# A recurrence and two expert layers on one core: another start list, a shorter unit, GpSimd in written order, spare PSUM for late conversions, a re-ordered last group

## The chip, the core and the metric

The kernel runs on one core of a Trainium2 chip. The core has five engines: TensorE (PE in the profile, PEld its weight loads), VectorE (DVE), ScalarE (ACT), GpSimd (POOL) and SyncE (SP), which issues most DMAs. The metric is device microseconds of one execution; before the change the median of 3 runs is 1033.3 us (1029.38 to 1034.28).

## The reference

Three stages follow one another. The first is a recurrence over 768 time steps for each of 4 x 8 heads with a 40 x 40 state; the second and third are dense layers on the 3072 x 320 result.

```python
for t in range(S):
    y[:, :, t] = np.einsum('bhd,bhde->bhe', rt, state)
    Sa = np.einsum('bhde,bhe->bhd', state, at)
    state_decay = state * wt[:, :, None, :] - np.einsum('bhd,bhe->bhde', Sa, bt)
    state = state_decay + np.einsum('bhd,bhe->bhde', vt, kt)
x = y.transpose(0, 2, 1, 3).reshape(B * S, H * D)
x = np.maximum(np.maximum(x @ w1, x @ w2), x @ w3) @ w_out     # 320 -> 768 -> 320
h = x @ w_in                                                   # 320 -> 2048
out = (h * np.tanh(np.log1p(np.exp(np.minimum(h, 20.0))))) @ w2_out   # h > 20: tanh(h)
```

The dense layers' weights come as 64-bit floats and are converted on the chip (`from64`: a test of the high words, then ScalarE, VectorE and GpSimd steps that put a 32-bit float together).

## The kernel before

**Recurrence.** The time axis is cut into 48 chunks of 32 steps (24 for each half of the batch). For two chunks at a time a *unit* (`pre`) makes what the chunk needs of its inputs alone: a scan of the decays on DVE (L281), its logarithm and inverse on ACT, the scaling of keys and b vectors on DVE (L310, L312), a product on POOL (L248), small matmuls on PE into `m` (L328), a copy of half of `m` to `ab` on ACT (L333), a transpose of the other half to `akT` on DVE (L336), and a masked selection on POOL (L343). In the generator `pre` a `yield` stands between the copy and the transpose. Four units make a batch, whose triangular systems are solved in 31 steps (`solve`: a product `tv`, L371, and a subtraction on `T`, L373): the first two batches on DVE, all others on POOL. A *chunk* (`chain`) is the serial part, five slots: `x0` (L449), `ups` (L462), `utps` (L472), the products into `cgps` (L416) with their mask `rs` on DVE (L483), and `ys` (L495) with the next state `sv` on DVE (L500). `kb` (L388) transposes a unit's keys on PE, four matmuls for each half, into one PSUM buffer that ACT empties into `ls` (L392).

**First dense layer.** It runs in 12 groups of 256 tokens beside the chunks. Products go to PSUM (`bps`, L743 to L747), the maximum of three is made by ACT and DVE (`mx`, L873, L875), its rounded part by ACT (`hh`, L877) and the rest by POOL (`hl`, L878); PE multiplies both by the second weights (L916), six pairs of `hh` and `hl` (hl0 to hl5) in a group, and ACT and DVE bring the result out (L905, L907). The generator of a group is advanced six times in a chunk.

**The order of the work.** Chunks 0 to 8 follow `START`, a list of 472 tokens written out: W, A, K, V and L are loads, u a step of a unit, c a slot of a chunk, e a solve step, w a step of a weight's conversion, k a half of `kb`, f a step of the first layer, m, s, l, Z memsets. There every engine and DMA queue works in that order. From chunk 9 `run` writes the order; PE, DVE and ACT keep it, while POOL and SP are ordered by the compiler's scheduler. In `run`, the solve steps of a batch are spread over the slots that are left to its due chunk (`steps` a slot).

**The tail.** After chunk 47 come the rest of the first layer's last groups together with conversions of the second layer's weights (`staged`, steps at L676 and L677 on DVE, L679 on POOL). `open_tail` gives the first layer a fourth PSUM bank. Then the second layer's six groups run (`Moe2.group`, 512 tokens each): 16 products `cps`, an activation chain on ACT and DVE (`e`, `r`, `gh`, `gl`), and 16 sets of output matmuls `cops` (L1093 to L1095). Then `gate.count` sums the counters of the range tests (matmul `g_p`, L171, reduction, cast to an integer `g_n`), and a branch on that number skips a general version of the program.

Of the kernel before, what the change touches and what calls it, by code (L numbers as in the profile page):

```python
# [17 lines left out]
C = 32  # L18
# [88 lines left out]
u4 w8 V2 c0 w11 w9 w13 u4 u5 w7 L2 w9 c1 A8 w8 w9 w10 w11 w10 k2 w14 w12 w10 u4 u5 x5 c1 w15 u5 w10 w11 u4 u4
w12 w16 c1 w13 w11 w12 w14 c1 w13 w17 w14 u4 w18 u4 w15 w13 c1 u5 w12 k3 V3 w14 u5 K7 w13 w15 w19 w14 u4 w16
u5 L3 w17 w17 u5 c2 w15 w16 w20 c2 u5 w18 c2 w15 w18 w19 u5 w17 w21 u5 c2 V4 c2 w18 k4 w17 u5 w19 w19 w20 c3
w18 w22 w23 w20 L4 w20 K8 w21 c3 w23 w19 w20 c3 w21 w23 w22 k5 w21 c3 w22 w23 w23 A9 u6 w21 V5 w16 c3 w16 L5  # L110
x6 w22 w22 c4 f20 u6 u6 c4 f21 u6 c4 u6 u6 u7 u7 c4 u7 V6 x7 f22 u6 u7 c4 K9 u7 u6 u6 u6 u6 L6 c5 f23 u7 u7 u7
# [11 lines left out]
class Gate:  # L123
# [26 lines left out]
    def count(self):  # L150
# [18 lines left out]
        with self.tc.tile_pool(name="g_ps", bufs=1, space=PSUM) as ps:  # L169
            p = ps.tile([1, len(runs)], F32, name="g_p")  # L170
            nc.tensor.matmul(out=p, lhsT=ones, rhs=cnt, start=True, stop=True)  # L171
            s = pool.tile([1, 1], F32, name="g_s")
            nc.vector.tensor_reduce(out=s, in_=p, op=ALU.add, axis=mybir.AxisListType.X)
# [5 lines left out]
class Attention:  # L179
# [93 lines left out]
    def pre(self, n):  # L273
# [60 lines left out]
        yield  # L334
# [255 lines left out]
    def run(self, fill):  # L590
# [333 lines left out]
class Moe2:  # L924
# [91 lines left out]
    def open_work(self, ctx):  # L1016
# [80 lines left out]
    def group(self, q):  # L1097

        tc, nc = self.tc, self.nc
        acc = self.acc = [self.psb.tile([128, DM], F32, name=f"cops{j}") for j in range(4)]  # L1100
        rest = iter(()) if q else self.conversions()
        under, self.begun = self.begun, []
        early = len(under)
        for m in range(16 + 3):
            if early <= m < 16 and (q, m) not in self.ps:
                self.product(q, m)
# [12 lines left out]
            with tc.issue_after(self.newest):  # L1119
                next(rest, None)  # L1120
                if m == 11:
                    finish(rest)
        del self.x[q]
        o = self.p2.tile([128, 4, DM], F32, name="o")
        ga, sb = divmod(2 * q, S // GT)
        for b2 in range(2):
            for i in range(2):
                j = 2 * i + b2
                if i:
                    nc.vector.tensor_copy(out=o[:, j], in_=acc[j])  # L1130
# [3 lines left out]
            nc.sync.dma_start(out=self.out[r0:r0 + 2 * GT].rearrange("(i p) d -> p i d", i=2), in_=o[:, b2:4:2])  # L1134
# [148 lines left out]
def program(tc, A, out, only=None):  # L1283
# [7 lines left out]
    with ExitStack() as c_mid:  # L1291
        keep = c_mid.enter_context(tc.tile_pool(name="keep", bufs=1, side="right"))
        moe2 = Moe2(tc, A, x1, out, gate)
        with ExitStack() as c_moe1:
            moe1 = Moe1(c_moe1, tc, A, xs, x1, gate)
            with ExitStack() as c_att:
# [5 lines left out]
                def fill(c, slot):  # L1302
# [18 lines left out]
                    if c >= HAND and (c > HAND or slot > 0) and slot in (1, 4):  # L1321
# [10 lines left out]
                with tc.manual_schedule(engines=IN_ORDER | {mybir.EngineType.Activation}):  # L1332
# [6 lines left out]
            moe1.open_tail()  # L1339
# [21 lines left out]
    n, total = gate.count()  # L1361
# [21 lines left out]
```

## Time and profile before

| | |
|---|---|
| runs shown | 1029.38, 1033.3, 1034.28 us |
| profiled execution, its own time | 1034.91 us |
| its span (first to last instruction) | 1033.2 us |
| TensorE clock granted, mean | 0.967 of full speed |
| busy: PE, DVE, ACT, POOL | 917.4, 752.2, 735.3, 479.4 us |
| chunk 0 starts, chunk 10 starts, second layer's steady part | 56.5, 206.9, 697 to 1016 us |

Busy shares are averages over stages with different limits. A chunk's length is read from one start of `x0` to the next; the clock column of the same stretch tells whether PE was slowed, and the idle time in brackets in front of an instruction tells what it waited for.

### The profile page before, as it was taken

The numbers are of one execution on the slowest core, as the hardware profiler recorded it, in microseconds if no ns is written. First come the engines' busy times: TensorE is split into PE (matmuls) and PEld (weight loads), VectorE is DVE, ScalarE is ACT, GpSimd is POOL, SyncE is SP. The second block draws the span as 40 slices with busy tenths as digits, with TensorE's granted clock in tenths as the row PEclk, the third lists the DMA queues.
The fourth block names the chain that finished last, engine by engine and source line by source line (L and its number), as shares of the span: only waits on it lengthen the run. The fifth ranks groups of instructions, "written<-read, shape, count | busy, mean of one in ns | idle before, by whom it ended". The sixth has DMA issues, their size and how long they took to land. (4 is left out here: it accounts for less than half of the span.)

```text
span 1033.2 us, 34141 instructions
## 1 busy us (share of the span) xinstructions
PE 917.4 (89%) x14098; PEld 824.6 (80%) x14098; DVE 752.2 (73%) x1411; ACT 735.3 (71%) x1858; POOL 479.4 (46%) x715
## 2 busy tenths in 40 slices
PE   3046778899999999999999999979999999999996
PEld 3034667798888888898988988969888999889985
DVE  8976788665564656565366666698998888898875
ACT  5466635575765667576688977878787978878874
POOL 8488706479659838963953434880202010020000
PEclk9999588899999999999999999989999999999999
DMA  9565522535354454445345454420100000000000
GB/s 233 148 182 160 134 51 65 152 95 150 92 139 118 114 148 106 118 113 139 94 129 151 124 140 150 118 66 1 57 1 31 26 32 26 24 33 1 26 1 29
DMA packets 117334, 96.07 MB, mean 93 GB/s; under 512 B 73316, under 2 KB 93412, under 8 KB 117172
## 3 DMA queue, kind: packets, MB, share of 16 engines
q1 hardware_dynamic: 116432, 93.59, 33.4%
q8 instruction: 113, 1.85, 0.8%
q14 instruction: 49, 0.40, 0.1%
q10 hardware_dynamic: 740, 0.23, 0.1%
HBM read 81.20 MB, written 12.58 MB: 91 GB/s over the span
## 5 line engine op out<-in xcount | busy, mean ns | idle before, releaser
L743 PE MATMUL bps<-bxh,bw 128*128 128x256 f32 x432 | 140.6, 326 | 4.5 <-ACT mx L873 3.4
L744 PE MATMUL bps<-bxl,bw 128*128 128x256 f32 x432 | 124.9, 289 | 3.1 <-DVE bxl L756 3.1
L745 PE MATMUL bps<-bxh,bw 128*128 128x256 f32 x432 | 123.7, 286 | 0.0
L1046 POOL CAST cxh<-cxl 128x512 fp32r<-128x512 f32 x15 | 13.1, 911 | 188.2 <-DMA cxl<-x 188.2
L743 PEld LDWEIGHTS bps<-bxh,bw 128*128 128x128 f32 x432 | 83.4, 193 | 13.3 <-ACT mx L873 4.0
L744 PEld LDWEIGHTS bps<-bxl,bw 128*128 128x128 f32 x432 | 84.2, 195 | 4.9 <-DVE bxl L756 4.9
L248 POOL TENSOR_TENSOR ax<-ax,pp 40x256 f32<-40x256 f32 x96 | 69.2, 739 | 37.1 <-DVE pp L281 24.0
L745 PEld LDWEIGHTS bps<-bxh,bw 128*128 128x128 f32 x432 | 84.1, 195 | 0.0
L483 DVE TENSOR_TENSOR rs<-cgps,cst 64x256 f32<-64x256 f32 x96 | 40.6, 423 | 58.2 <-PE cgps L416 56.1
L878 POOL TENSOR_TENSOR hl<-mx,hh 128x256 fp32r<-128x256 f32 x72 | 56.0, 779 | 52.6 <-ACT hh L877 46.4
L1089 DVE TENSOR_TENSOR gl<-e,gh 128x512 fp32r<-128x512 f32 x93 | 69.9, 752 | 14.4 <-ACT gh L1088 13.4
L500 DVE TENSOR_TENSOR sv<-ys,pp 40x320 f32<-40x320 f32 x92 | 44.9, 488 | 47.3 <-PE ys L495 45.8
L875 DVE TENSOR_TENSOR mx<-bps,mx 128x256 f32<-128x256 f32 x144 | 60.2, 418 | 24.6 <-ACT mx L873 13.7
L373 POOL TENSOR_TENSOR T<-T,tv 128x31 f32<-128x31 f32 (+15 forms) x124 | 73.7, 594 | 8.6
L916 PE MATMUL bps<-hh,bo 128*128 128x256 f32 x360 | 77.0, 296 | 0.6 <-ACT mx L873 0.6
L1077 ACT ACTIVATE e<-e 128x512 f32<-128x512 f32 x93 | 58.6, 630 | 25.4 <-DVE e L1075 25.0
L1081 DVE SCALAR_TENSOR_TENSOR e<-e,r 128x512 f32<-128x512 f32 x93 | 68.6, 737 | 8.7 <-ACT r L1079 8.6
L495 PE MATMUL ys<-rs,ls 128*40 128x72 f32 x1536 | 66.9, 247 | 8.5 <-DVE rs L483 4.2
L371 POOL TENSOR_TENSOR tv<-tr,T 128x31 f32<-128x31 f32 (+15 forms) x124 | 67.8, 547 | 11.1 <-DVE tr L364 2.6
L343 POOL TENSOR_SCALAR_AFFINE_SELECT ax<-akT 32x256 f32<-32x256 f32 x96 | 47.5, 494 | 51.5 <-DVE akT L336 47.3
L495 PEld LDWEIGHTS ys<-rs,ls 128*40 128x40 f32 x1536 | 58.0, 130 | 15.1 <-issue 4.9
L1074 ACT ACTIVATE e<-cps 128x512 f32<-128x512 f32 x93 | 54.7, 589 | 18.9 <-PE cps L747 18.8
(241 smaller groups left out, 3157.2 us busy)
## 6 DMA issues: line engine op xcount, KB each, us to landing
bk<-in_KB_dram SPq DMA_DIRECT2D x24, 448.0 KB
sv<-in_SV_dram SPq DMA_DIRECT2D x96, 80.0 KB
raw<-in_w_dram SPq DMA_DIRECT2D x18, 384.0 KB
again<-in_w_dram SPq DMA_DIRECT2D x27, 256.0 KB
w<-in_W_dram SPq DMA_DIRECT2D x21, 231.0 KB
v<-in_VT_dram SPq DMA_DIRECT2D x48, 96.0 KB
rs<-in_RT_dram SPq DMA_DIRECT2D x48, 96.0 KB
cxl<-x SPq DMA_DIRECT2D x12, 384.0 KB
```

Source lines behind the costliest of these rows:

```text
L248: self.nc.gpsimd.tensor_tensor(out=xv[:, h], in0=xv[:, h], in1=P[ro, h, 0:C], op=ALU.mult)
L371: eng.tensor_tensor(out=tv, in0=abT[:, s, s + 1:C].unsqueeze(2).to_broadcast([128, n, s + 1]), in1=T[:, s, 0:s + 1].unsqueeze(1).to_broadc ...
L373: eng.tensor_tensor(out=T[:, s + 1:C, 0:s + 1], in0=T[:, s + 1:C, 0:s + 1], in1=tv, op=ALU.subtract)
L495: nc.tensor.matmul(out=self.ys[64 * y:64 * y + 40, p, 0:72], lhsT=l[:, y, p], rhs=r_[:, :, 4 * (p % 4) + 2 * (1 - y) + p // 4], start=True ...
L743: nc.tensor.matmul(out=ps, lhsT=h[:, k], rhs=xh[:, k], start=(k == 0), stop=False)
L744: nc.tensor.matmul(out=ps, lhsT=h[:, k], rhs=xl[:, k], start=False, stop=False)
L745: nc.tensor.matmul(out=ps, lhsT=l[:, k], rhs=xh[:, k], start=False, stop=False)
L875: after(1, lambda ps=ps, mx=mx: nc.vector.tensor_tensor(out=mx, in0=ps, in1=mx, op=ALU.max))
L916: nc.tensor.matmul(out=pss[d][rows], lhsT=lhsT, rhs=rhs, start=first, stop=last)
L1077: nc.scalar.activation(out=e, in_=e, func=AF.Square, bias=1.0)
L1081: nc.vector.scalar_tensor_tensor(out=e, in0=e, scalar=1.0, in1=r, op0=ALU.add, op1=ALU.mult)
L1089: nc.vector.tensor_tensor(out=gl, in0=e, in1=gh.bitcast(F32), op=ALU.subtract)
```

## The change

The change makes seven edits.

1. Another START list: the same 472 tokens, permuted. W0 is the first load and K0 the ninth token; before, K0 was the first. In chunk 9 the two halves of `kb`, k10 and k11, no longer follow one another directly.
2. In `pre`, the `yield` between L333 and L336 stays only while START is being written out. In `run` a unit has one step fewer, and `akT` is issued a slot earlier.
3. In `run`, a batch gets no solve step in slot 0 of a chunk whose number divides by 4.
4. POOL keeps the written order in `run` too, and the DMAs `again` are held in program order only there.
5. Past the last chunk, the first layer has three PSUM banks, and the fourth bank becomes the tile `words`, which takes the result of L676 and is read by L677.
6. The last group of the second layer makes its products a step earlier from m = 12, counts inside the group ahead of the output copies, gives three of four output copies to ACT and one to DVE, and sends one of the last two output DMAs from ACT's queue.
7. A condition in `tests` is written with the number 9 in place of HAND, which is 9.

```diff
 START = """
-m0 m1 K0 W0 W1 A0 W2 m2 A2 A1 K1 W3 K2 m3 A3 s1 V0 K3 w0 w1 w2 l1 s0 C l0 p R1 R0 u0 u0 u1 x0 u1 x1 u0 u0 u0
+W0 m1 m2 m0 W1 A2 A0 W2 K0 W3 V0 A1 K1 s0 K2 C m3 A3 s1 K3 w0 w1 w2 l1 p u0 u1 x0 u0 R0 u0 u0 u1 u0 u0 u0 R1
...
-    def count(self):
+    def count(self, psum):
...
+        p = psum[0:1, 0:len(runs)]
+        nc.tensor.matmul(out=p, lhsT=ones, rhs=cnt, start=True, stop=True)
...
         nc.scalar.copy(out=self.ab[:, i:i + 8], in_=psv[:, :, C:2 * C])
-        yield
+        if self.written:
+            yield
         akT = p1.tile([128, 4, 2, C], F32, name="akT")
...
                     steps = -(-left // max(1, 5 * (due - c) - slot - 2))
+                    if c > HAND and c % 4 == 0 and slot == 0:
+                        steps = 0
...
         self.tail = True
-        self.banks.append(self.pool("b_pt", 1, space=PSUM))
+        return self.pool("b_pt", 1, space=PSUM).tile([128, 512], I32, name="words")
...
-            self.tc.keep_in_program_order(dma)
+            if self.free:
+                self.tc.keep_in_program_order(dma)
...
-            if early <= m < 16 and (q, m) not in self.ps:
-                self.product(q, m)
+            for p in (m, m + 1)[:1 + (last and m >= 12)]:
+                if early <= p < 16 and p not in made:
+                    self.product(q, p)
+                    made.add(p)
...
+        if last:
+            self.passed = self.gate.count(self.psa.tile([128, self.N], F32, name="cps"))
...
-                if i:
+                if i and not (last and b2):
                     nc.vector.tensor_copy(out=o[:, j], in_=acc[j])
...
-                with tc.manual_schedule(engines=IN_ORDER | {mybir.EngineType.Activation}):
+                moe1.free = True
+                with tc.manual_schedule(engines=IN_ORDER | {mybir.EngineType.Activation, mybir.EngineType.Pool}):
...
-            moe1.open_tail()
+            moe2.stage.psum = moe1.open_tail()
...
-    n, total = gate.count()
+    n, total = moe2.passed
```

How the change moves instructions is shown at three places. The first is POOL around chunk 20, where the solve of a batch (`tv` and `T`) and the `hl` of a group of the first layer alternate. Before:

```order
L371 TENSOR_TENSOR tv_5364<-tr1_174,T0_161 128x255
L878 TENSOR_TENSOR hl4_4685<-mx_5162,hh4_4679 128x256
L373 TENSOR_TENSOR T0_161<-T0_161,tv_5364 128x17x15
L371 TENSOR_TENSOR tv_5413<-tr1_174,T0_161 128x256
L373 TENSOR_TENSOR T0_161<-T0_161,tv_5413 128x16x16
L371 TENSOR_TENSOR tv_5454<-tr1_174,T0_161 128x255
L373 TENSOR_TENSOR T0_161<-T0_161,tv_5454 128x15x17
L878 TENSOR_TENSOR hl5_4686<-mx_5303,hh5_4680 128x256
```

With the change:

```order
L883 TENSOR_TENSOR hl4_4687<-mx_5164,hh4_4681 128x256
L371 TENSOR_TENSOR tv_5364<-tr1_174,T0_161 128x255
L373 TENSOR_TENSOR T0_161<-T0_161,tv_5364 128x17x15
L883 TENSOR_TENSOR hl5_4688<-mx_5303,hh5_4682 128x256
L371 TENSOR_TENSOR tv_5451<-tr1_174,T0_161 128x256
L373 TENSOR_TENSOR T0_161<-T0_161,tv_5451 128x16x16
L371 TENSOR_TENSOR tv_5454<-tr1_174,T0_161 128x255
L373 TENSOR_TENSOR T0_161<-T0_161,tv_5454 128x15x17
```

hl4 now stands ahead of the step with 255 elements instead of in the middle of it, and hl5 two solve steps (four instructions) earlier than it did.

The second is DVE in chunk 17, where the first layer's split (L755, L756), its copy to the output (L907) and a unit's `akT` follow one another. Before:

```order
L755 TENSOR_SCALAR bxh,g_t<-bxl 128x768
L756 TENSOR_TENSOR bxl<-bxl,bxh 128x768
L907 TENSOR_TENSOR mx<-bps,mx 64x256
L336 STREAM_TRANSPOSE akT<-m_3558 128x2x4x32
L464 COPY ud<-ups 128x4x40
```

With the change:

```order
L757 TENSOR_SCALAR bxh,g_t<-bxl 128x768
L758 TENSOR_TENSOR bxl<-bxl,bxh 128x768
L336 STREAM_TRANSPOSE akT<-m_3558 128x2x4x32
L912 TENSOR_TENSOR mx<-bps,mx 64x256
L464 COPY ud<-ups 128x4x40
```

`akT` now stands ahead of the copy to the output, which has line L912 in the changed file.

The third is PE in chunk 9: the transposes of keys `kb`, and the first layer's `bps`. Before:

```order
L747 MATMUL bps<-bxl,bw_107 128x256
L472 MATMUL utps<-cst,ud 128x128 x2
L743 MATMUL bps<-bxh,bw_108 128x256
L744 MATMUL bps<-bxl,bw_108 128x256
L745 MATMUL bps<-bxh,bw_108 128x256
L743 MATMUL bps<-bxh,bw_108 128x256
L744 MATMUL bps<-bxl,bw_108 128x256
L745 MATMUL bps<-bxh,bw_108 128x256
L746 MATMUL bps<-bxh,bw_108 128x256
L747 MATMUL bps<-bxl,bw_108 128x256
L388 MATMUL kb<-cst,bk_150 128x104 x8
L416 MATMUL cgps<-rs_167,uT 32x32
```

With the change:

```order
L388 MATMUL kb<-cst,bk_150 128x104 x4
L472 MATMUL utps<-cst,ud 128x128 x2
L745 MATMUL bps<-bxh,bw_108 128x256
L746 MATMUL bps<-bxl,bw_108 128x256
L747 MATMUL bps<-bxh,bw_108 128x256
L745 MATMUL bps<-bxh,bw_108 128x256
L746 MATMUL bps<-bxl,bw_108 128x256
L747 MATMUL bps<-bxh,bw_108 128x256
L748 MATMUL bps<-bxh,bw_108 128x256
L749 MATMUL bps<-bxl,bw_108 128x256
L388 MATMUL kb<-cst,bk_150 128x104 x4
L416 MATMUL cgps<-rs_167,uT 32x32
```

The eight transposes that stood in one run are now two runs of four, with one `utps` and eight matmuls of the first layer between them.

## Rows read from the trace of the kernel before

**Rows 1.** Stretches of the span: busy time by engine, PEclk granted clock, DMA share.

```profile
100.80:155.00 54.20, 39.96 (x909) 34.84 (x912) 43.96 (x98) 29.40 (x87) 22.34 (x36) 0.72 0.40 97
697.00:1016.00 319.00, 318.66 (x1759) 287.14 (x1760) 278.20 (x456) 264.36 (x455) 29.80 (x25) 1.00 0.06 21
```

**Rows 2.** PE's waits, chunks 10 to 47 (206 to 624 us): total, times, longest.

```profile
PE kb L388 <- DVE akT L336: 4.0, 5, 1.0
PE bps L916 <- POOL hl L878: 3.2, 3, 1.5
...
PE cgps L416 <- ACT uT L475: 2.5, 3, 1.4
```

**Rows 3.** The same columns, single chunks: 9, 14, 15, 17, 18 and 20.

```profile
188.30:206.90 18.60, 15.46 (x327) 13.62 (x322) 10.72 (x20) 9.83 (x29) 6.76 (x11) 0.82 0.53 140
252.00:266.90 14.90, 13.10 (x283) 11.61 (x282) 5.91 (x13) 6.65 (x23) 13.63 (x24) 0.89 0.33 82
266.90:277.50 10.60, 10.60 (x227) 9.79 (x226) 7.44 (x13) 8.95 (x25) 9.16 (x18) 1.00 0.43 121
288.60:302.30 13.70, 12.38 (x231) 11.14 (x234) 10.05 (x18) 10.08 (x31) 7.70 (x16) 0.88 0.42 114
302.30:313.20 10.90, 10.90 (x287) 9.99 (x288) 5.82 (x13) 6.76 (x22) 9.89 (x17) 1.00 0.47 113
323.80:337.90 14.10, 12.68 (x283) 11.53 (x282) 6.46 (x14) 6.28 (x21) 13.06 (x19) 0.88 0.47 132
```

**Rows 4.** Timeline of POOL in chunk 20: start, duration, line, operation, tiles.

```profile
326.17 0.73 POOL L878 TENSOR_TENSOR hl<-mx,hh 128x256 fp32r<-128x256 f32 x1
...
328.08 0.62 POOL L371 TENSOR_TENSOR tv<-tr,T 128x256 f32<-128x256 f32 x1
328.78 0.73 POOL L373 TENSOR_TENSOR T<-T,tv 128x256 f32<-128x256 f32 x1
...
330.93 0.72 POOL L878 TENSOR_TENSOR hl<-mx,hh 128x256 fp32r<-128x256 f32 x1
```

**Rows 5.** Timeline of PE, chunks 17 and 20; idle time and releaser in brackets.

```profile
292.15 0.55 PE L388 MATMUL kb<-cst,bk 104*128 104x104 f32 x4 [1.02 <-DVE akT L336]
...
331.70 0.38 PE L916 MATMUL bps<-hl,bo 128*128 128x256 f32 x1 [1.42 <-POOL hl L878]
```

**Rows 6.** Timeline of DVE in chunk 17.

```profile
291.09 0.42 DVE L907 TENSOR_TENSOR mx<-bps,mx 64x256 f32<-64x256 f32 x1 [1.13 <-ACT mx L905]
```

**Rows 7.** Timeline of POOL in chunk 12.

```profile
230.47 1.19 POOL L878 TENSOR_TENSOR hl<-mx,hh 128x256 fp32r<-128x256 f32 x1
...
234.70 0.73 POOL L878 TENSOR_TENSOR hl<-mx,hh 128x256 fp32r<-128x256 f32 x1
```

**Rows 8.** Timeline of ACT in chunk 14.

```profile
258.96 0.37 ACT L873 COPY mx<-bps 128x256 f32<-128x256 f32 x1 [3.91 <-POOL hl L878]
```

**Rows 9.** Timeline of PE in chunk 9.

```profile
194.56 0.57 PE L388 MATMUL kb<-cst,bk 104*128 104x104 f32 x4 [0.64 <-DVE akT L336]
197.63 0.95 PE L388 MATMUL kb<-cst,bk 104*128 104x104 f32 x4 [2.50 <-ACT ls L392]
```

**Rows 10.** DVE's waits up to chunk 10 (0 to 206 us).

```profile
DVE rs L483 <- PE cgps L416: 9.9, 5, 4.4
...
DVE pp L281 <- DMA w<-in_W_dram: 1.5, 1, 1.5
```

**Rows 11.** Line L676 in the whole run: min/median/max ns, first and last start.

```profile
L676 DVE TENSOR_SCALAR bits<-raw x24: 485/552/561, 23.5 to 105.2; 128x384 int32<-128x384 int32 x18, 128x320 int32<-128x320 int32 x6
...
L676 DVE TENSOR_SCALAR t<-raw x13: 328/599/1424, 641.8 to 689.1; 128x320 int32<-128x320 int32 x7, 128x384 int32<-128x384 int32 x6
```

**Rows 12.** PE's waits between chunk 47 and MoE2's groups (624 to 700 us).

```profile
PE bps L916 <- POOL hl L878: 2.5, 1, 2.5
```

**Rows 13.** Timeline of the end.

```profile
1023.16 0.41 PE L1093 MATMUL cops<-c_cw,gh 128*128 128x320 f32 x1 [1.34 <-ACT gh L1088]
...
1026.54 0.14 DVE L175 CAST g_n<-g_s 1x1 int32<-1x1 f32 x1
```

More of the change, by code (lines that the diff above doesn't have):

```diff
@@ L107 @@
[L107 to L111, printed above, removed]
@@ new lines @@
+u2 x1 u2 l0 u1 u1 u2 u0 x2 u1 u1 u0 u1 u0 u0 u1 u1 u3 x3 u3 l2 u2 u2 u2 L0 u1 u3 u1 u3 z6 u3 u3 u2 u2 u2 u3 w0
+w3 L1 u2 u2 u3 w1 w1 u3 e0 w0 w4 w5 u3 z4 u3 z5 w2 K4 e0 A5 e0 w1 e0 e0 e0 A6 z7 e0 U A4 e0 w0 w0 A7 w2 w3 e0
+e0 w6 e0 e0 e0 w1 w4 w3 w3 w5 K5 e0 e0 e0 e0 e0 e0 w3 e0 e0 e0 w7 w2 w2 w4 w4 w5 w4 w6 e0 k0 k1 e0 w6 D w8 w5
+e0 w5 r K6 w9 w10 e0 V1 e0 e0 e0 e0 e0 e0 e0 e0 c0 w7 w7 Z0 c0 u4 w8 w8 u4 c0 w9 w11 w12 x4 w7 c0 u4 u4 w9 Z1
+w8 V2 w13 w11 c0 u4 w7 w8 L2 w9 c1 A8 w6 w11 w6 u5 w10 w10 u4 k2 w12 w10 x5 w13 u5 u5 u5 w10 w12 u4 u4 w14 w11
@@ new lines @@
+w11 w13 c1 c1 w9 c1 w15 w16 w17 u4 u4 w13 w13 V3 w14 w14 w18 w12 k3 w12 u5 u5 w15 c1 L3 w17 w15 w19 w14 w16 c2
+c2 w14 u4 w15 w18 w18 u5 c2 w17 w19 u5 w15 w16 w20 w21 c2 V4 w19 w18 u5 w17 u5 w19 w20 w18 u5 w22 w17 c2 k4
+w23 w20 c3 A9 L4 c3 w20 w21 w23 w19 w21 c3 w20 w22 w23 w22 w22 w21 k5 w23 c3 V5 w21 u6 w16 w22 w16 c3 L5 w23
+K7 c4 f20 u6 u6 c4 x6 u6 c4 u6 f21 u6 u7 u7 K8 c4 u7 u7 u6 c4 L6 u6 u7 u6 u6 x7 V6 u6 c5 u7 u7 u7 f22 f23 u7
+A10 f24 f25 K9 c5 u7 u7 e1 e1 e1 e1 e1 e1 c5 c5 e1 f26 f27 e1 e1 e1 V7 f28 k6 c5 L7 e1 e1 e1 e1 c6 c6 e1 c6 e1
@@ L168, in count @@
         nc.vector.memset(ones, 1.0)
[L169 to L173, printed above, removed]
+        p = psum[0:1, 0:len(runs)]
+        nc.tensor.matmul(out=p, lhsT=ones, rhs=cnt, start=True, stop=True)
+        s = pool.tile([1, 1], F32, name="g_s")
+        nc.vector.tensor_reduce(out=s, in_=p, op=ALU.add, axis=mybir.AxisListType.X)
         n = pool.tile([1, 1], I32, name="g_n")
@@ L802, in weights @@
             yield from64(self.nc, self.tmp, self.A["wo"][j], 1, DM, self.gate, lambda t, j=j: self.put_out(t[:, 0], j), later=True)
+    free = False
     def tests(self):
@@ L1099, in group @@
         tc, nc = self.tc, self.nc
+        last = q == 5
         acc = self.acc = [self.psb.tile([128, DM], F32, name=f"cops{j}") for j in range(4)]
@@ L1103, in group @@
         early = len(under)
+        made = {p for r, p in self.ps if r == q}
         for m in range(16 + 3):
-            if early <= m < 16 and (q, m) not in self.ps:
-                self.product(q, m)
+            for p in (m, m + 1)[:1 + (last and m >= 12)]:
+                if early <= p < 16 and p not in made:
+                    self.product(q, p)
+                    made.add(p)
             for i, g in enumerate(under):
@@ L1133, in group @@
             r0 = (2 * ga + b2) * S + sb * GT
-            nc.sync.dma_start(out=self.out[r0:r0 + 2 * GT].rearrange("(i p) d -> p i d", i=2), in_=o[:, b2:4:2])
+            (nc.scalar if last and b2 else nc.sync).dma_start(out=self.out[r0:r0 + 2 * GT].rearrange("(i p) d -> p i d", i=2), in_=o[:, b2:4:2])
 def any64(nc, pool, src, n, cols, out):
@@ L1320, in fill @@
                         next(groups, None)
-                    if c >= HAND and (c > HAND or slot > 0) and slot in (1, 4):
+                    if c >= 9 and (c > 9 or slot > 0) and slot in (1, 4):
                         next(tests, None)
```

12 lines of the change are left out of this document (4 added, 8 removed).

## The prediction

> **What bounds the kernel now.** I read the busy time by stretches first. From 697 us to 1016 us PE is busy 318.66 of 319 us at full clock [rows 1]; the change leaves the order there as it is, so these 319 us stay. Nothing that spares DVE, ACT or POOL there can be seen in the time. In the start it is otherwise: between 100.8 and 155 us PE is busy 39.96 of 54.2 us, and the clock column says 0.72 [rows 1], a mixture of the levels of 1.2 and 2.4 GHz. So there a gap costs twice: itself, and the slow work after it.
>
> The second view is PE's waits for chunks 10 to 47. Waits of PE are few: 4.0 us for `akT`, 3.2 us for `hl`, 2.5 us for `uT` [rows 2]. The third view, single chunks, tells what they cost. Chunks 15 and 18 have no gap, a clock of 1.00, and last 10.60 and 10.90 us; these I take as the floors of odd and even chunks. Chunks 14, 17 and 20 last 14.90, 13.70 and 14.10 us at 0.88 or 0.89 [rows 3]: 4.0, 3.1 and 3.2 us above them. Chunk 17 has one gap of 1.02 us in front of `kb`, chunk 20 one of 1.42 us in front of L916 [rows 5]. Here 2.44 us of gap go with 6.3 us of time, and the clock column says where the other 3.9 us are.
>
> **The change, part by part.** The profiled execution is the base: 1034.91 us, 1.7 us more than its span, 1.6 us over the median of the runs shown.
>
> *The unit's step.* In chunk 17, `akT` stands behind L907, which starts at 291.09 after DVE had waited 1.13 us for ACT [rows 6]; PE's `kb` waits for `akT`, since the buffer it needs is free only then [rows 5]. With `akT` ahead of L907, DVE does it in that idle time: 1.13 and 0.42 us earlier, more than the 1.02 us of the gap. What is late next is L907 by some 0.45 us, and its output transfer has nobody close behind. All five `kb` gaps, 4.0 us [rows 2], should go.
>
> *POOL in written order and no solve step in slot 0 of every fourth chunk.* At chunk 20 hl4 starts at 326.17 and hl5 at 330.93, after three pairs of solve instructions, one of which takes 0.62 + 0.73 = 1.35 us [rows 4]. hl5 is two pairs earlier after the change: 2 x 1.35 = 2.7 us, less what hl4's new place shifts (nothing: both stand ahead). The gap it ends is 1.42 us [rows 5]. So the two long `hl` gaps go, 2.9 of the 3.2 us [rows 2].
>
> Together 4.0 + 2.9 = 6.9 us of gaps. For the two chunks shown I take the measured 6.3 us; the remaining 4.5 us of gaps I price at 1.5 us for each, since among them one is as long as that of chunk 20 and the rest are 1 us or less: 6.7 us. That is **-13 us**. The bounds: at 1.0 for each us -6.9, at the ratio of 6.3 to 2.44 -17.8.
>
> *The first batch on POOL.* In chunk 14, ACT's copy `mx` waits 3.91 us for an `hl` that POOL has put behind other work [rows 8], PE then for ACT, and the chunk lasts 4.0 us over its floor. In written order that `hl` is done sooner. But in chunk 12 the fifth and sixth `hl` of a group, at 230.47 and 234.70 now [rows 7], come behind several more solve pairs of 1.35 us; I place them at about 236 and 238 us (an estimate from those rows), some 2 to 4 us after PE wants them. I take one new gap of 2 us with 1.5 us of slow clock against 4.0 us gained: **-0.5 us**, between -4.0 (no new gap) and +4 (the gap is 4 us at the same price, twice).
>
> *The list.* W0 goes first. DVE waits 1.5 us for it at its first scan [rows 10], behind K0's transfer, and DVE is what fills the start: -1.5 us. In chunk 9 `kb` waits 0.64 us for `akT` and, for its second half, 2.50 us for ACT, which must first empty the one buffer behind a logarithm and an exponential [rows 9]. The chunk lasts 18.6 us at 0.82 [rows 3], 8 us over the odd floor. With eight matmuls between the halves ACT has that time; I count half of the 8 us: -4. What the rest of the permutation does to the waits of the start the trace can't tell. DVE's largest there is `rs` for `cgps`, 9.9 us in five [rows 10]: half of it more or less is the bound on either side. **-5.5 us**, between -15 (the whole 8 us, 1.5, and half of 9.9) and +5.
>
> *The tail.* Three banks instead of four let PE's products wait sooner for ACT's copies. Most of this would be absorbed where PE waits 2.5 us for `hl` anyway [rows 12]. And L676 writes PSUM. Thirteen such steps lasted 328 to 1424 ns in SBUF, with a median of 599, while 24 steps that wrote PSUM (`bits`) lasted 485 to 561, with a median of 552 [rows 11]. The spread is what a neighbour makes of it, and the PSUM form has next to none. By medians 13 x 0.047 = 0.6 us of DVE are saved, and more where long steps stand in a chain. I take **-1 us**, between -4 and +3.
>
> The Trainium skill (VectorE: DVE Perf Modes, section "Why PSUM operands drop a tier") says that an operand in PSUM keeps VectorE from using both of its SBUF read ports for one tensor, so that 32-bit data goes at the plain rate: by it `words` makes each of these steps slower than the 328 ns form. The rows agree as far as they show: 552 against 328 ns at the shortest. By that rule alone the sum would get 13 x 0.22 = 2.9 us of DVE more, not 0.6 less; against it stands the median of 599 ns, which the SBUF form has beside busy neighbours. The same skill (SBUF, State Buffer, section "Who interferes with whom") calls the ports that VectorE shares with GpSimd an exclusive lock, which fits a maximum of 1424 ns.
>
> *The end.* PE waits 1.34 us for the last `gh` [rows 13]; with products one step ahead, the last activation chain runs under matmuls: -1.3. The count's cast now ends at 1026.68 us, and 6.5 us follow in which no view shows an instruction: the read of the number, the branch and the last transfers. With the count ahead, the read can begin where the last set of `cops` ends. That set of 12 matmuls begins at 1023.16 [rows 13]; at 319 us for 6 x 16 sets with their products, a set's own part is under 2 us [rows 1], so the read begins near 1025.1, 1.6 us sooner: -1.6. Together **-2.9 us**, between -1.3 (the last output's transfer sets the end) and -4.
>
> Sum: -13 - 0.5 - 5.5 - 1 - 2.9 = -22.9, so 1034.9 - 22.9 = 1012 us; less 1.6 us to stand at the median: I take **1010 us**.
>
> **The rivals.**
> - *`hl` held back by solve steps in every batch.* The scheduler could slip `hl` between solve instructions when its data was there; in written order it can't. POOL is busy 13.06 of 14.1 us in chunk 20 [rows 3], so it has hardly any slack. If POOL lags behind the written slot by more than 2 to 3 us at hl4, chunks 12, 20, 28 and 36 get the gap of chunk 12 (about 5 us with the clock) and, behind it, that of chunk 14 (4.0 us): 4 x 9 = 36 us, less the 11 us that such gaps cost now, less some 10 of the other gains: 1034.9 + 15 = **1050 us**. Against it: the empty slot 0 gives POOL two pairs of room just there, and POOL is at 9.89 of 10.9 us in chunk 18.
> - *The gaps move on.* What PE no longer waits for at `kb` and L916 it waits for at `uT` (2.5 us now [rows 2]) or at the split of the first layer; the chunk is bound by its own serial slots. Then the end's 2.9 us and the start's first 1.5 to 4 remain: **1028 us**. For it: ACT's copies and POOL are both close to full in these chunks. Against it: chunks 15 and 18 reach the floor with the same work.
> - *The list does more.* Half of the start's clock loss and DVE waits go too: -18 instead of -5.5: **999 us**. For it: PE is busy only 39.96 of 54.2 us at 0.72 between 100.8 and 155 us. Against it: the steps of chunks 0 to 8 stand at nearly the same places of the list.
> - *The tail gets worse.* `words` is one tile, so each conversion's L676 waits for the L677 before it, and three banks hold PE up: +7 instead of -1, **1019 us**.
>
> **How the numbers follow.** A measurement of this kernel tells 0.5%, 5.2 us, from no change. The forecast has 0.54, held-back `hl` 0.08, moved gaps 0.14, a better list 0.16, a worse tail 0.08. Faster than 1028.1: nearly all of forecast, list and tail, and a third of the moved gaps, 0.80; slower than 1038.5: the held-back `hl` and a little for a list that lengthens the start, 0.09; 0.11 between. With the terms' ends all on one side the sum would be 990 or 1039; the ends are not met together, so I take the better list on one side and the moved gaps on the other: 997 to 1028 us, which leaves out the held-back case and a few hundredths at each end.
>
> **What would show it.** Right: no wait of `kb` for `akT` after 206 us; chunks 17 and 20 at 11 us and clock 1.00; chunk 9 without its 2.50 us gap; the last `cops` set without the 1.34 us; `g_n` ahead of the output copies. The new gap of chunk 12 should stand there as L916 waiting for `hl`. Wrong: `hl` waits of over 2 us in chunks 20, 28 and 36, a chunk 0 that starts later than 56.5 us, or a second layer that starts as late as now though the chunks are shorter.

## The result and the profile after

The changed kernel takes 1020.81 us (1019.93 to 1021.82, 4 runs) against 1033.74 us (1029.38 to 1034.28, 4 runs), a ratio of 0.9884 with an interval of 0.9856 to 0.9913. That is 12.9 us less, inside the range of 997 to 1028, and a little over half of what was forecast. Its profiled execution took 1021.82 us, with a span of 1020.1.

The table cuts the spans of both profiles at the same places: the first `x0` matmul of chunks 10, 16 and 47, the end of the last `cops` matmul, and the end.

| us | start to chunk 10 | chunks 10 to 15 | chunks 16 to 46 | chunk 47 to last `cops` | to the end |
|---|---|---|---|---|---|
| before | 206.93 | 70.58 | 346.40 | 401.27 | 8.02 |
| changed | 206.54 | 73.83 | 336.03 | 397.37 | 6.34 |
| difference | -0.4 | **+3.3** | **-10.4** | -3.9 | -1.7 |

So chunks 16 to 46 gain, the first batch of chunks loses, and the start gives nothing in this execution. In the start DVE waits less for W0, but now it waits for the keys, whose load K0 was the first load before and is the ninth token now. DVE's waits up to 57 us in the changed kernel, to be held against the 1.5 us of [rows 10]:

```profile
DVE bk L309 <- DMA bk<-in_KB_dram: 2.1, 1, 2.1
...
DVE pp L280 <- DMA w<-in_W_dram: 0.4, 1, 0.4
```

Chunk 0 begins at 56.86 us, 0.4 us later than before. PE's waits in chunks 10 to 47 of the changed kernel, with the columns of [rows 2]:

```profile
PE bps L921 <- POOL hl L883: 4.8, 1, 4.8
...
PE cgps L416 <- ACT uT L475: 1.4, 3, 0.6
```

The line of `kb` for `akT`, 4.0 us in five [rows 2], is gone, and the waits for `hl` have become a single one of 4.8 us. Single chunks, with the columns of [rows 3] (9, 12, 14, 17 and 20):

```profile
190.50:206.50 16.00, 13.97 (x323) 12.79 (x322) 11.46 (x20) 10.37 (x31) 8.31 (x10) 0.89 0.60 156
...
228.50:248.00 19.50, 14.72 (x284) 13.19 (x282) 5.82 (x11) 6.00 (x20) 17.46 (x25) 0.74 0.31 86
...
258.80:269.70 10.90, 10.90 (x284) 10.00 (x282) 6.32 (x14) 6.81 (x23) 9.70 (x19) 1.00 0.45 112
291.40:302.80 11.40, 11.04 (x227) 9.87 (x226) 9.73 (x17) 9.42 (x29) 8.08 (x16) 1.00 0.56 150
325.10:336.00 10.90, 10.90 (x284) 10.02 (x282) 5.97 (x12) 5.96 (x20) 10.15 (x14) 1.00 0.57 152
```

Chunks 14, 17 and 20 have lost their long gaps and their slow clock. Chunk 12 had no long gap in the kernel before:

```profile
228.60:240.20 11.60, 11.28 (x283) 10.17 (x282) 6.14 (x13) 6.62 (x22) 10.82 (x16) 1.00 0.55 151
```

Now it lasts 19.5 us at 0.74, with POOL busy 17.46 us of it. The timeline of POOL there, in the changed kernel, shows why:

```profile
229.44 3.62 POOL L247 TENSOR_TENSOR ax<-ax,pp 40x256 f32<-40x256 f32 x4
...
237.36 0.72 POOL L883 TENSOR_TENSOR hl<-mx,hh 128x256 fp32r<-128x256 f32 x1
...
239.38 0.72 POOL L883 TENSOR_TENSOR hl<-mx,hh 128x256 fp32r<-128x256 f32 x1
```

The two `hl` that started at 230.47 and 234.70 us [rows 7] now start at 237.36 and 239.38 us, behind solve steps and the product L247. PE waits for the first of them (timeline of PE, changed kernel):

```profile
238.14 0.58 PE L921 MATMUL bps<-hl,bo 128*128 128x256 f32 x1 [4.78 <-POOL hl L883]
```

The new first words of the conversions in the tail, against the row of `t<-raw` in [rows 11] (line L678 of the changed file). Eleven of the thirteen steps write PSUM; the last two stay in SBUF, and the longest, 1421 ns, is the same step as the one of 1424 ns before:

```profile
L678 DVE TENSOR_SCALAR words<-raw x11: 481/497/561, 633.0 to 658.8; 128x320 int32<-128x320 int32 x6, 128x384 int32<-128x384 int32 x5
L678 DVE TENSOR_SCALAR t<-raw x2: 896/1158/1421, 666.2 to 675.9; 128x384 int32<-128x384 int32 x1, 128x320 int32<-128x320 int32 x1
```

The step behind it reads these words. Line L677 before, L679 in the changed kernel:

```profile
L677 DVE SCALAR_TENSOR_TENSOR t<-raw,t x13: 476/546/987, 642.2 to 691.9; 128x320 int32<-128x320 int32 x7, 128x384 int32<-128x384 int32 x6
...
L679 DVE SCALAR_TENSOR_TENSOR t<-raw,words x11: 471/489/555, 634.2 to 662.0; 128x320 int32<-128x320 int32 x6, 128x384 int32<-128x384 int32 x5
```

And the end of the changed kernel, where the idle time in front of the last `cops` set [rows 13] is gone and the output copies are the last work that shows:

```profile
1011.75 0.42 PE L1099 MATMUL cops<-c_cw,gh 128*128 128x320 f32 x1
...
1013.38 1.08 ACT L1144 COPY o<-cops 128x320 f32<-128x320 f32 x3 [1.68 <-PE cops L1101]
1013.67 0.49 DVE L1142 COPY o<-cops 128x320 f32<-128x320 f32 x1 [1.25 <-PE cops L1101]
```

### The profile page after: what moved, and what is told of

Its sections match the earlier page's. It is cut to its first block, busy times and chain, and to the rows that moved or that the text cites. A ratio compares the mean times of both kernels' runs of the same rounds, so it can differ in the third digit from the quotient of the medians.

```text
span 1020.1 us, 34113 instructions
## 1 busy us (share of the span) xinstructions
PE 916.0 (90%) x14098; PEld 825.4 (81%) x14098; DVE 748.2 (73%) x1410; ACT 736.0 (72%) x1859; POOL 476.5 (47%) x715
## 4 chain that ended last, share of the span: by engine, by line
PE 72%; DVE 12%; ACT 7%; DMA 3%; POOL 3%; issue 3%; SPq 0%; ACTq 0%; DVEq 0%; POOLq 0%
PE bps L745 6%; PE bps L921 5%; PE cops L1099 5%; PE cops L1100 5%; PE cops L1101 5%; PE ys L495 5%; PE bps L746 4%; PE cps L745 4%; PE bps L747 4%; PE cps L746 4%; PE cps L747 4%; PE cgps L416 2%; PE m L327 2%; PE ups L462 2%; PE bps L748 2%
## 5 line engine op out<-in xcount | busy, mean ns | idle before, releaser
L247 POOL TENSOR_TENSOR ax<-ax,pp 40x256 f32<-40x256 f32 x96 | 68.8, 736 | 21.3 <-PE m L327 5.6
L1095 DVE TENSOR_TENSOR gl<-e,gh 128x512 fp32r<-128x512 f32 x93 | 68.4, 735 | 12.1 <-ACT gh L1094 12.1
L1087 DVE SCALAR_TENSOR_TENSOR e<-e,r 128x512 f32<-128x512 f32 x93 | 69.3, 745 | 9.7 <-ACT r L1085 9.4
L495 PE MATMUL ys<-rs,ls 128*40 128x72 f32 x1536 | 64.4, 243 | 8.6 <-ACT bw L690 4.8
L1088 DVE SCALAR_TENSOR_TENSOR e<-e,r 128x512 f32<-128x512 f32 x93 | 68.2, 733 | 0.9
```

Of the source, the lines that this page charges most:

```text
L247: self.nc.gpsimd.tensor_tensor(out=xv[:, h], in0=xv[:, h], in1=P[ro, h, 0:C], op=ALU.mult)
L495: nc.tensor.matmul(out=self.ys[64 * y:64 * y + 40, p, 0:72], lhsT=l[:, y, p], rhs=r_[:, :, 4 * (p % 4) + 2 * (1 - y) + p // 4], start=True ...
L1087: nc.vector.scalar_tensor_tensor(out=e, in0=e, scalar=1.0, in1=r, op0=ALU.add, op1=ALU.mult)
L1088: nc.vector.scalar_tensor_tensor(out=e, in0=e, scalar=-float(np.sqrt(8.0)), in1=r, op0=ALU.add, op1=ALU.mult)
L1095: nc.vector.tensor_tensor(out=gl, in0=e, in1=gh.bitcast(F32), op=ALU.subtract)
```

## The experiments

All kernels are the changed one with one thing undone or altered. The table has their profiles cut as above, and the medians of their runs; the expectations stand below, each with its edit (old_list, order16_old_list and alternate_old_list also take the whole START list of before, which is left out).

| run | to chunk 10 | 10 to 15 | 16 to 46 | 47 to last `cops` | to the end | median us |
|---|---|---|---|---|---|---|
| changed | 206.54 | 73.83 | 336.03 | 397.37 | 6.34 | 1020.81 |
| after_again | 202.97 | 73.45 | 336.17 | 395.91 | 6.61 | 1019.08 |
| even_first | 204.96 | 77.42 | 335.90 | 396.41 | 6.26 | 1020.2 |
| alternate_old_list | 202.99 | 74.33 | 334.53 | 396.10 | 6.24 | 1016.89 |
| pool_sched | 206.91 | 67.55 | 341.79 | 396.27 | 6.14 | 1019.06 |
| order16 | 204.63 | 67.55 | 336.09 | 396.03 | 6.44 | **1011.34** |
| order16_old_list | 205.01 | 67.33 | 334.65 | 396.56 | 6.61 | **1009.87** |
| slot0 | 205.94 | 74.69 | 339.93 | 397.00 | 6.19 | 1022.07 |
| long_unit | 209.83 | 75.06 | 342.29 | 396.90 | 6.19 | 1028.9 |
| old_list | 205.15 | 73.61 | 334.91 | 397.13 | 6.13 | 1018.71 |
| four_banks | 202.99 | 73.56 | 335.40 | 398.67 | 6.18 | 1018.86 |
| no_words | 205.17 | 73.54 | 336.66 | 398.53 | 6.22 | 1023.95 |
| old_count | 205.39 | 73.85 | 337.11 | 396.02 | 8.06 | 1022.93 |

**after_again**, the changed kernel itself, timed beside others.

> The changed kernel itself, beside the runs that follow, to see what the start alone varies by. So far chunk 10 began between 203.0 and 206.9 us in six profiles that share the START list and the unit's step of the changed kernel. Theory: that is variation between executions and not the edits: time 1018 to 1022 us, chunk 10 between 203 and 207 us, chunk 12 at 19 to 20 us.

1019.08 us (1016.81 to 1020.65), ratio 0.9868 (0.9846 to 0.9890). Chunk 10 begins at 202.97 us, 3.6 us before the first profile of the same program, the two columns of chunks behind it agree within 0.4 us, and the column from chunk 47 differs by 1.5 us. So medians of these kernels can be read to some 2 us, the column up to chunk 10 to some 4 us, and the column from chunk 47 to some 1.5 us. Chunks 16 to 46 take 335.40 to 337.11 us in the seven profiles that share the new list and the order from chunk 16 on, so that column too is read to some 1.5 us; single chunks tell more.

**long_unit**, the unit's step as before:

```diff
-        if self.written:
-            yield
+        yield
```

> The changed kernel with the unit's step back (the yield between the ab copy and akT). Theory: the kb gaps of before come back in chunks 17, 21, 25, 29 and 33: 2.2, 0.6, 0.8, 0.6 and 0.6 us that these chunks lost, so about +4.8 us, time about 1025.5, and PE waits for akT of about 4 us. Rival (written order on POOL had taken those gaps, since POOL's selections wait for akT): no kb gap over 0.3 us after 206 us, time within 1 us of 1020.8.

The waits of `kb` came back (PE's waits from chunk 9 on, long_unit):

```profile
PE kb L387 <- DVE akT L335: 3.6, 7, 0.8
...
PE kb L387 <- ACT ls L391: 2.5, 1, 2.5
```

It costs 8 us or more, not 4.8: 6.3 us in chunks 16 to 46, 1.2 in chunks 10 to 15, and 2.7 in chunk 9. The five chunks of the expectation, 17, 21, 25, 29 and 33, have 3.1 us of it, chunk 28 has 1.5; the rest is spread. The window of chunk 9 then reads:

```profile
191.10:209.80 18.70, 15.63 (x323) 13.89 (x322) 10.53 (x21) 10.36 (x31) 5.56 (x9) 0.82 0.49 133
```

against 16.00 us in the changed kernel. The 2.5 us wait of `kb` for `ls` in chunk 9, which the prediction gave to the list, is the unit's: it is there with either list and the long unit (before, long_unit) and in neither with the short one. In old_list, too, the halves of `kb` stand apart in chunk 9, at 193.19 and 194.72 us. The description of the first edit puts this down to the new list; it came with the second.

**old_list**, the START list of before in the changed kernel.

> The changed kernel with the START list of before. Theory: the list moved chunk 10's start by only 0.4 us, so the time stays within 1.5 us of 1020.8, with chunk 7 some 3 us shorter and chunk 9 some 2.6 us longer. Rival (the list was what the other edits need, since it sets how far POOL and DVE are when the written order of chunk 9 begins): chunk 10 starts 3 us or more later than 206.5, or chunk 12's gap changes by over 2 us, time 1025 or more.

The wait list of PE in chunk 9 of old_list is one row, the same as that of the changed kernel there:

```profile
PE m L327 <- POOL ax L247: 2.0, 1, 2.0
```

Chunk 9 lasts 16.5 us, chunk 12 has its gap (5.1 us), and chunk 10 begins at 205.15 us, in the middle of the nine starts that share the new list and the short unit (202.97 to 206.91). The median is 2.1 us below that of the changed kernel, and chunk 9 is 0.4 us longer, not 2.6. The new list gives nothing that can be seen, and the losses that the rival expected did not come. The table even speaks a little against the list: in chunks 16 to 46 the three kernels with the list of before and the written order from chunk 16 on take 334.53 to 334.91 us, all seven with the new list 335.40 or more. Why a list that ends with chunk 8 should matter there was not traced.

**pool_sched**, POOL ordered by the scheduler from chunk 9 on:

```diff
-                with tc.manual_schedule(engines=IN_ORDER | {mybir.EngineType.Activation, mybir.EngineType.Pool}):
+                with tc.manual_schedule(engines=IN_ORDER | {mybir.EngineType.Activation}):
```

> The changed kernel with POOL ordered by the scheduler again from chunk 9 on (slot 0 of every fourth chunk still without solve steps). Theory: written order made the 4.8 us gap of chunk 12 and took away the 4.0 us of chunk 14: chunk 12 back to about 11.6 us, chunk 14 about 14.9. The skipped slot may already save chunks 20 and 28 (then they stay at 10.9 us, and the time is about 1018) or not (14.2 us each, time about 1024.5). Rival: chunk 12's gap stays at over 4 us because the skipped slot, not the order, pushed the steps together.

The chunks 12, 14, 20 and 28 of pool_sched:

```profile
228.90:240.50 11.60, 11.15 (x283) 10.08 (x282) 5.42 (x11) 5.92 (x19) 10.74 (x16) 1.00 0.53 141
252.10:263.30 11.20, 11.18 (x283) 10.12 (x282) 6.32 (x15) 6.66 (x23) 10.34 (x17) 1.00 0.44 109
318.40:333.20 14.80, 12.68 (x283) 11.43 (x282) 5.83 (x12) 5.92 (x19) 13.69 (x20) 0.88 0.44 118
409.44:422.85 13.41, 11.20 (x284) 10.08 (x283) 5.90 (x12) 5.99 (x19) 12.47 (x18) 1.00 0.42 107
```

Chunk 12's gap belongs to the written order; chunks 20 and 28 need it. The 4.0 us of chunk 14, though, are gone here too, so they were not the order's to give. Which edit took them was not tried; the unit's shorter step is the likely one, since the unit's product on POOL, which starts at 254.37 us in the kernel before, ahead of the late `hl`, starts at 250.94 us here, before chunk 14 begins. Written order on POOL costs 6.3 us in chunks 10 to 15 and gives 5.8 us in chunks 16 to 46: nothing in all, which is what the medians say (1019.06 and 1020.81).

**slot0**, without the rule on slot 0:

```diff
-                    if c > HAND and c % 4 == 0 and slot == 0:
-                        steps = 0
```

> The changed kernel without the rule that leaves slot 0 of every fourth chunk free of solve steps. hl5 then stands behind one more pair of solve instructions, 1.35 us. In the changed kernel hl5 was ready at 330.95 us in chunk 20, and PE reached it some 0.7 us later. Theory: a gap of about 0.6 us each in chunks 20 and 28, 11.5 to 12 us instead of 10.9, and chunk 12 a little longer: time about 1022 us. Rival (the rule did the work, the order none): chunks 20 and 28 back at 14 us, time 1027 or more.

Two of its waits in chunks 18 to 32, and chunk 20 (chunk 28 reads alike):

```profile
PE bps L919 <- POOL hl L881: 1.8, 2, 0.9
...
PE m L327 <- issue: 1.3, 2, 0.9
```

```profile
325.20:337.30 12.10, 11.21 (x283) 10.07 (x282) 6.03 (x12) 6.04 (x20) 11.24 (x16) 1.00 0.52 137
```

Two gaps of 0.9 us, as one pair of 1.35 us less a margin of 0.5 us makes them (the expectation had read 0.7), at a price of 1.2 us each. The column from 16 to 46 is 3.9 us longer, but chunk 32 has 1.2 us of that, by a gap of 0.9 us in which PE waited for nothing that the profile shows ("issue"); the changed kernel has such a gap in chunk 18, and after_again none. So 2.3 us in chunks 20 and 28 are shown for the rule. Neither it nor the order does alone what both do: chunk 20 lasts 14.8 us with the rule and the scheduler's order, 12.1 with the written order and no rule, 10.9 with both.

**even_first**, the first batch with fewer solve steps early:

```diff
-                    steps = -(-left // max(1, 5 * (due - c) - slot - 2))
+                    slots = max(1, 5 * (due - c) - slot - 2)
+                    steps = max(1, left // slots) if due == 16 else -(-left // slots)
```

> The changed kernel, but the first batch on POOL (due at chunk 16) gets left // slots solve steps a slot, at least one, instead of the rounded-up number. Theory: the 4.8 us gap of chunk 12 comes from two solve steps a slot in front of hl4 and hl5; with one a slot both hl are about six pairs (some 7 us) earlier, chunk 12 goes from 19.5 to about 11 us at clock 1.00, and the time from 1020.8 to about 1012.5 us. Rival (POOL is late for another reason: its slow products L247 and selections L343 beside DVE): hl still comes after 236 us, chunk 12 stays over 15 us, time 1017 to 1021. A second price is open: the steps left for chunks 14 and 15 may come late for chunk 16, then x0 there waits for T.

Chunks 12 and 15 of even_first:

```profile
226.50:237.40 10.90, 10.90 (x284) 10.02 (x282) 5.76 (x12) 5.92 (x20) 9.07 (x13) 1.00 0.57 152
259.50:282.30 22.80, 14.24 (x228) 13.08 (x226) 8.51 (x15) 10.00 (x29) 18.00 (x35) 0.70 0.24 64
```

The steps in front of `hl` made the gap: without them chunk 12 is at its floor. But the open price was paid in full. DVE waits for the solved system at the end of chunk 15 (DVE's waits, even_first), and `rs`, the next instruction on DVE, waits along; PE waits 5.9 us for it:

```profile
DVE tr L377 <- POOL T L373: 6.7, 1, 6.7
```

**alternate_old_list**, the steps spread evenly, with the list of before:

```diff
-                    steps = -(-left // max(1, 5 * (due - c) - slot - 2))
+                    slots = max(1, 5 * (due - c) - slot - 2)
+                    steps = left // slots if due == 16 and slot % 2 == 0 else -(-left // slots)
```

> The changed kernel with the START list of before, and the first batch on POOL spread evenly: the rounded-down number of solve steps in slots 0, 2 and 4, the rounded-up number in 1 and 3. Theory: chunk 12's gap and the late T at chunk 15 are the two ends of one spread; between them there is room. hl4 comes three pairs (4 us) earlier, the gap of chunk 12 is under 1 us and chunk 12 lasts 11 to 12 us, T is ready for chunk 16, and the time is 1018.7 - 7.5 = about 1011 us. Rival (POOL has no room for the first batch at all): chunk 12 or chunk 15 or 16 still loses over 4 us, time 1015 or more.

Chunk 12 was 12.2 us and T came in time, but chunk 14 lasted 18.4 us at 0.81: there `hl` stood behind solve steps, ACT's `mx` waited 6.0 us for it (ACT's waits, chunk 14), and PE for ACT.

```profile
ACT mx L879 <- POOL hl L884: 6.0, 1, 6.0
```

The rival was right in the loss and the time, at a chunk that it had not named. In written order none of the three spreads tried is without a loss: 73.8, 77.4 and 74.3 us for chunks 10 to 15.

**order16**, POOL in written order from chunk 16 on only:

```diff
-            if c == HAND:
+            if c in (HAND, 16):
                 yield
...
+                with tc.manual_schedule(engines=IN_ORDER | {mybir.EngineType.Activation}):
+                    next(chunks)
```

> The changed kernel with POOL ordered by the scheduler up to chunk 15 and in written order from chunk 16 on. Theory: written order pays in the later batches and costs in the first; chunks 10 to 15 take 67.5 us as with the scheduler (73.8 in the changed kernel), chunks 20 and 28 stay at 10.9 us, time about 1014.5 us. Rival (one order needs the other: the scheduler leaves POOL in another state at chunk 16): chunks 16 to 22 lose what was won, time 1018 to 1021.

1011.34 us, ratio 0.9771 (0.9734 to 0.9807), 3 us better than expected, with four runs from 1008.69 to 1015.59. The chunks are what each order gave alone: 67.55 us for the first batch, 336.09 us for the others. Chunks 12 to 15 and 20:

```profile
226.60:238.30 11.70, 11.25 (x284) 10.08 (x282) 5.50 (x12) 6.01 (x20) 10.84 (x16) 1.00 0.55 143
238.30:249.80 11.50, 10.79 (x227) 9.85 (x226) 8.37 (x17) 9.39 (x29) 10.64 (x16) 1.00 0.54 148
249.80:261.10 11.30, 11.28 (x285) 10.13 (x283) 6.43 (x15) 6.69 (x23) 10.44 (x17) 1.00 0.42 101
261.10:272.10 11.00, 10.71 (x227) 9.87 (x226) 7.47 (x15) 9.37 (x26) 10.01 (x21) 1.00 0.43 116
316.10:327.10 11.00, 11.00 (x283) 10.07 (x282) 6.01 (x12) 6.00 (x19) 10.21 (x15) 1.00 0.53 143
```

POOL is over 90% busy in four chunks in a row, so with this little slack the order counts. In order16 the unit's product L247 runs at 222.30 us, ahead of chunk 12, and the two `hl` start 0.1 and 6.1 us into that chunk; in the changed kernel L247 runs inside it, and they start 8.8 and 10.8 us into it. That the solve can wait, since nobody needs it before chunk 16, is the reading of these orders; even_first shows where the waiting ends.

**order16_old_list**, the same with the list of before.

> Written order on POOL from chunk 16 on and the START list of before, with the other edits. Theory: the new list gives nothing: within 2 us of 1011.3, rather below, 1010 us; chunk 10 begins between 203 and 206 us. Rival (the new list pays once chunk 12's gap no longer hides it): 1013 or more.

1009.87 us, ratio 0.9778 (0.9754 to 0.9801): as order16, and better than both kernels of this study. The new list again gives nothing.

**four_banks** and **no_words**, two steps back in the tail: the first gives the fourth bank to the first layer and has no `words`, the second leaves that bank unused (its first `+` line is `pass`).

```diff
-        return self.pool("b_pt", 1, space=PSUM).tile([128, 512], I32, name="words")
+        self.banks.append(self.pool("b_pt", 1, space=PSUM))
...
-            moe2.stage.psum = moe1.open_tail()
+            moe1.open_tail()
```

> The changed kernel with the fourth PSUM bank given to the first layer again and the conversions' first words in SBUF, as before. Theory (the words make the tail's conversions shorter): PE's 2.5 us wait for hl comes back, the tail from chunk 47 on is about 2.4 us longer, time about 1023. Rival (the wait went because POOL and DVE meet in another order after a shorter run): tail as long as in the changed kernel, time within 1 us of 1020.8.

> The changed kernel with three PSUM banks for the first layer and the conversions' first words in SBUF, the fourth bank unused. It tells the bank from the words. Theory: three banks alone cost up to 2 us and the words give them back with more: the tail is longer than in the changed kernel by 2 to 4 us, time about 1023 to 1025. Rival (three banks are what helps, since the products then don't run ahead of POOL): time as in the changed kernel.

From chunk 47 to the last `cops` they take 398.67 and 398.53 us; all profiles with `words` take 395.91 to 397.37. The two are alike, so the bank costs nothing that this column can tell, and the words give 1.2 to 2.8 us. In four_banks PE's old wait is there again (PE's waits in the tail, four_banks, to be held against [rows 12]):

```profile
PE bps L921 <- POOL hl L883: 2.5, 1, 2.5
```

In no_words it is 1.3 us, in the changed kernel none. The time is not won where the prediction looked for it. The first eleven steps of L678 take 5.69 us together in four_banks and 5.39 in no_words, where they write SBUF, and 5.70 in the changed kernel, where they write PSUM. It is the next step, L679, that is shorter when its words come from PSUM:

```profile
L679 DVE SCALAR_TENSOR_TENSOR t<-raw,t x13: 479/546/1035, 629.8 to 678.5; 128x320 int32<-128x320 int32 x7, 128x384 int32<-128x384 int32 x6
```

Its first eleven take 7.79 us in four_banks (of this row), 7.12 in no_words and 5.68 in the changed kernel. These 1.4 to 2.1 us of DVE are of the size of the gain; that they are the gain is argued and not shown. The medians, 1018.86 and 1023.95, lie on both sides of the changed kernel's, and the profiled executions began chunk 10 at 202.99 and 205.17 us; here the column decides and not the median.

**old_count**, the count behind the last group again, in a PSUM pool of its own.

```diff
-        if last:
-            self.passed = self.gate.count(self.psa.tile([128, self.N], F32, name="cps"))
...
-    n, total = moe2.passed
+    n, total = gate.count()
```

> The changed kernel with the count behind the last group again, in a PSUM pool of its own; products ahead, copies and the output DMA from ACT stay. Theory: from the last cops matmul to the end of the span 8.0 us as before instead of 6.3, so +1.6 us, about 1022.4. Rival (the last output's transfer or something else sets the end): 6.3 us, no change.

8.06 us from the last `cops` matmul to the end, against 6.13 to 6.61 in the twelve profiles with the early count, so the count was worth 1.7 us. With the count last, the end of the span comes 6.5 us (before) and 6.8 us (old_count) after the cast of `g_n`. In the changed kernel the cast ends at 1007.86 us, 12 us before the end, so something else sets the end there; no view shows what.

## Why the prediction was right and where it was not

The sum was -22.9 us; the profiled execution moved by -13.1. The time fell inside the range because the range is 31 us wide and the costly rivals did not come: the terms for the first batch on POOL and for the list missed by 3.8 and 5.1 us. The tail gave 2.9 us more than counted, by another step than the one named, which is luck. Term by term:

- **The unit's step: the mechanism was right.** All waits of `kb` for `akT` went. long_unit puts the edit at 6.3 us in chunks 16 to 46, 1.2 in 10 to 15 and 2.7 in chunk 9, more than the 4.0 us of its gaps.
- **"For the two chunks shown I take the measured 6.3 us; the remaining 4.5 us of gaps I price at 1.5 us for each": too high by 2.6 us.** Chunks 16 to 46 gave 10.4 us where this term said 13. Chunks 20 and 28, with the `hl` gaps, gave 6.5 us, priced at 5.4; the five with a `kb` gap gave 4.8, priced at 7.6; chunks 18 and 23 lost 0.8 and 0.7. What failed is the floor of 10.60 us for all odd chunks: with their gaps gone the five last 11.2 to 11.8 us, so chunk 17 won 2.2 us and not 3.1. On the price of a gap: where the chunk kept the clock at 1.00 it cost little more than its own length, or less where another wait took over (slot0: 1.2 us for 0.9; chunk 28 of pool_sched: 2.5 us for 2.2; chunk 21: 0.6 us for 1.0). With a slow clock behind it, it cost about twice its length (3.3 us for 1.42 in chunk 20, 3.9 for 2.1 in chunk 20 of pool_sched, 8.5 for 4.78 in chunk 12 of the changed kernel), but only 1.4 times in chunk 15 of even_first (12.2 us for two gaps of 8.6).
- **"I take one new gap of 2 us with 1.5 us of slow clock against 4.0 us gained": wrong by 3.8 us.** The place and the times of both `hl` were right (236 and 238 us estimated, 237.36 and 239.38 measured), but the gap was 4.78 us and chunk 12 grew from 11.6 to 19.5 us. Chunks 10 to 15 lost 3.3 us where the term said -0.5, near its bound of +4; chunks 12 and 14 alone make +3.9 (7.9 lost, 4.0 gained). And the 4.0 us of chunk 14 were gone in pool_sched too, where the scheduler orders POOL: that gain needed no written order.
- **The list, -5.5 us: the largest error.** -0.4 us in the profile, nothing in old_list. "With eight matmuls between the halves ACT has that time" described the right gap and gave it to the wrong edit; the order of the changed kernel showed the halves apart, but not which edit had parted them. The 1.5 us at the first scan were not won either: DVE waits 0.4 us for W0, but 2.1 us for the keys, and chunk 0 starts 0.4 us later, which the prediction had named as a sign of being wrong. Chunk 9 is 2.6 us shorter, the unit's doing, but chunk 7, 19.6 to 20.7 us in the four profiles with the list of before, lasts 22.4 to 23.4 us in the ten with the new one, so that chunk 10 begins much as before.
- **The tail, -1, and the end, -2.9.** -3.9 and -1.7 us together, -5.6 against -3.9. `words` gave some 2 us, old_count 1.7 us for the count; the 1.34 us in front of the last set are gone [rows 13], and PE has no wait left in the last group. The reason given for `words` was wrong, as four_banks and no_words show: the steps that write PSUM take no less time together; the steps that read it do. What the tail gained beyond these is some 0.6 us in this profile, 1.3 us by four_banks and no_words (398.6 against 401.27), and was not traced.

Of the rivals, held-back `hl` came true at one place of four, chunk 12; chunks 20, 28 and 36 stayed at their floors, since POOL's lag there was below the point named (in chunk 20 hl5 was ready 0.5 us ahead of PE). Moved gaps, a better list and a worse tail did not come. On `words` the two figures weighed there compared unlike sets: the 599 ns are the median of all thirteen steps, of which two, the longest among them, were not moved. Of the eleven that were, the median rose from 413 ns before (417 in four_banks, 431 in no_words) to 497 ns, as the rule of the Trainium skill has it (VectorE: DVE Perf Modes, "Why PSUM operands drop a tier"), and the longest fell from 990 to 561 ns; their sum, 5.70 us, is no smaller than in four_banks (5.69) and no_words (5.39). So the rule held for the median step, and the tail was shorter all the same, with a shorter next step.

## What to carry to other kernels

Where an engine is over 90% busy for several stages, a written order on it is a bet on each place where urgent short work stands behind long work that nobody needs yet; let a priority decide there, and write the order down only where there is slack: order16 got 6.3 us more than the change itself in chunks 10 to 15 from such an edit (9.5 us by the medians, of which the rest lies where both have the same order). When several edits change one order, undo each alone before a move is put down to one of them. Price a gap by the clock of its stretch, and against the length that the same chunk reaches without it: at 1.00 it cost about its own length, with the slow clock behind it 1.4 to 2.3 times that. And where a step is made to write elsewhere, time the step that reads it too.

## What was not expected of the hardware

The clock column is not the clock where the trace holds no record of it. Chunk 4 in two executions of the same program, changed and after_again:

```profile
110.90:121.80 10.90, 8.26 (x234) 6.71 (x234) 7.40 (x13) 7.94 (x25) 8.03 (x13) 1.00 0.70 165
```

```profile
110.90:121.80 10.90, 8.26 (x234) 6.71 (x234) 7.40 (x13) 7.96 (x25) 8.04 (x13) 0.50 0.71 174
```

The column differs by the full two levels, and the chunk's length and PE's busy time do not differ at all. But the clock records of the first trace begin at 137.1 us, and those of the second at 101.3; ahead of them the column reads 1.00. PE's own pace tells the level. Here are the 32 matmuls of `ys` in chunks 4 and 5 of the changed kernel (timeline of PE):

```profile
118.55 2.15 PE L495 MATMUL ys<-rs,ls 128*40 128x72 f32 x32 [0.50 <-issue]
...
137.52 1.20 PE L495 MATMUL ys<-rs,ls 128*40 128x72 f32 x32
```

They take 2.15 us in chunk 4, as in after_again at 0.50, and 1.20 us in chunk 5, where the records have begun and say 1.00. It is 2.15 us in chunk 4 of all fourteen profiles, the kernel before among them, and chunk 4 lasts 10.9 us in all. So it ran at the low level every time, and whether a gap in the start "costs twice", as the prediction says, was not tried by any run.

Where both traces have records, the same program did get different levels in the same chunk. Chunk 9, 16.05 us at 0.89 in the changed kernel's profile, reads in after_again:

```profile
188.40:202.97 14.57, 12.53 (x324) 11.40 (x323) 11.11 (x20) 10.38 (x31) 8.30 (x10) 1.00 0.62 165
```

Chunk 7 lasts 23.38 us at 0.78 and 22.37 at 0.85. These two chunks hold 2.5 of the 3.6 us by which chunk 10 begins apart; what decides between the levels was not tried.
